# Loading a chunk's decays with it, and clearing the experts' places one expert per step

## The chip, the cores and the metric

The kernel runs on one core of one Trainium2 chip. The metric is the device time of one execution in microseconds (us). Five engines work side by side, each in its own program order: TensorE (PE in the profile, its weight loads PEld), VectorE (DVE), ScalarE (ACT), GpSimd (POOL) and SyncE (SP). Transfers are issued by SP, ACT and POOL, each into a queue of its own (the rows SPq, ACTq and POOLq show the issuing), and are carried by 16 DMA engines that all queues share.

## The reference

Three parts follow each other on 2304 tokens (4 sequences of 576) of width 512, all in float32.

```
scores = scale * q @ k^T                  # 8 heads of 64, per sequence
ret    = (scores * gamma_h ** (i - j) for j <= i, else 0) @ v
x      = ret, heads side by side                      # [2304, 512]
expert = argmax(normalise(x) @ normalise(emb).T / tau)    # one of 8
x      = gate * (relu(x @ w1[expert]) @ w2[expert])
out    = (silu(x @ w_gate) * (x @ w_val)) @ w_out
```

The factor gamma ** (i - j) is the decay. It splits into a mask inside a block of positions and powers of gamma between blocks.

## The kernel before, in words

**Attention in chunks.** Each sequence is cut into five chunks of 128, 128, 128, 128 and 64 positions, so there are 20 steps in the first stage, about the first 120 us of the span. `load_chunk(i)` brings q, k, k by rows and v of chunk i into one of six buffers `ck`: 1024 KB for a full chunk and 512 KB for the short one. `qk(i)` multiplies k and q on TensorE (line 234) and VectorE multiplies the scores by the mask `dmask_s` (line 237). `prep_chunk(i)` lets GpSimd multiply q by the decays `dq_s` (line 219, result `qd`) and k by its own powers (line 222). `pv(i)` multiplies by the state carried from earlier chunks (line 247) and by v (line 251), and ScalarE copies the result to `xT` (line 253). `state(i)` updates the carried state (line 268), which ScalarE copies to `sbd` (line 271). `rows(i)` turns the chunk back into token rows and gets the router's values (lines 280 to 287).

**Order of a step.** The order is written out by hand. In step i TensorE does `qk(i)`, `pv(i-1)`, `state(i-1)` (from the second sequence on `state(i)`) and `rows(i-2)`; step 1 also has four small transposes (line 549). The load of chunk i+5 is issued in step i, once the buffer of chunk i-1 is free. Fifteen products of ones (`warm`, line 523) stand ahead of step 0.

**The experts' places.** Tokens are sent row by row (514 floats: 512 of x, token number, gate) to a table `xs` in memory, where expert e owns a stretch of rows. Each expert later reads its first 320 rows whether they hold tokens or not, so those 8 x 320 rows are cleared first. In step 3 GpSimd fills a tile `zt` of rows with zeros and a token number behind the last token, and ScalarE issues three transfers (line 597) that write 128, 128 and 64 rows to each of the eight experts: 2056, 2056 and 1028 KB. The first tokens are sent in step 7.

**Counters of the transfers.** The transfers of SP and ACT take eight counters (DMAHW0 to DMAHW7) in turn, in the order in which the program states them, over both queues. A transfer is issued only after the previous one on its counter has landed, so it waits for the transfer eight places earlier. This wait stands on the issuing engine: on ACT it would hold the engine's arithmetic too.

**After the stage.** The eight experts (lines 681 to 712) and the gated feed-forward (lines 765 to 806) follow, both on TensorE, with weights loaded and split ahead by the same engines. The change does not touch them.

Of the kernel before, what the change touches and what calls it, by code (L numbers as in the profile page):

```python
# [4 lines left out]
F32 = mybir.dt.float32  # L5
# [4 lines left out]
ALU = mybir.AluOpType  # L10
# [20 lines left out]
# the upper word of the float64 2**-126, read as a float32  # L31
TINY = 2.0 ** -15 * 1.125
# weights come in units [128, 2, 512]: eight per expert, then three per pair of feed-forward columns
# (gate, value, output); they are kept in a ring of places
# [3 lines left out]
# products of ones that keep TensorE's clock up: before the first load is there, while the last chunk's  # L38
# experts are found, and while the tokens go through memory to the first expert
WARM = (15, 5, 42)  # L40
NTP = NT + CAP
# small constants, packed by columns
SMALL = dict(
    keep=dict(ident=P, base=E, rows=E, pos=NTI, below=E * E),
    small=dict(dk=4 * H, r8=E, tok=B * NC_ + NTI, tau=1),
# [3 lines left out]
def build(tc, main, tail, emb, wexp, dmask, dq, keep, small, lim, wffn, out):  # L49
# [24 lines left out]
    # ---------------------------------------------------------------- weights  # L74
    # Each unit is kept as hi + lo, two float32r parts that sum to it exactly. A step loads, or
    # splits, a unit of an expert or half a unit of the feed-forward's float64 weights.
# [18 lines left out]
    def split_step():  # L95
# [11 lines left out]
        else:  # L107
            # float64 bits: the float32 with their sign, exponent and leading 23 fraction bits is put
            # together from the two words, and is zero where they are below float32's least normal
# [21 lines left out]
    def feed(count=1, done=None, ahead=True):  # L131
        """Split up to `count` pieces, as far as the ring has room, with loads running ahead;
        `done`: the units that are behind us by now."""
        if done is not None:
            prog["done"] = done
        for c in range(count + 1):
            while ahead and prog["load"] < min(prog["split"] + RAW, len(steps)):
                load_step()
            if c == count or prog["split"] == len(steps) or steps[prog["split"]][0] >= prog["done"] + RING:
                return  # L140
            split_step()

    # ---------------------------------------------------------------- attention and routing
# [10 lines left out]
    dq_s = ac.tile([P, NP, S - P], F32, name="dq_s")  # L154
# [11 lines left out]
    zt = ac.tile([P, NTI, XW], F32, name="zt")  # L166
# [4 lines left out]
    sps = {}  # L171

    def load_chunk(i):
        b, c = divmod(i, NC_)
        t = cq.tile([P, 4, NP * P], F32, tag="ck", name="ck")
        if c < NC_ - 1:
            src = main[b, c].rearrange("p (a n) -> p a n", a=4)
            if i == 0:
                for h in range(2):
                    s = slice(256 * h, 256 * h + 256)  # L180
                    nc.sync.dma_start(out=t[:, 0:2, s], in_=src[:, 0:2, s])
                nc.sync.dma_start(out=dmask_s, in_=dmask)
                nc.scalar.dma_start(out=emb_s, in_=emb)
                nc.scalar.dma_start(out=small_s, in_=small)
                ck["raw0"] = t
            elif i == 1:
                nc.sync.dma_start(out=t[:, 0:2], in_=src[:, 0:2])
                nc.sync.dma_start(out=ck.pop("raw0")[:, 2:4], in_=main[0, 0].rearrange("p (a n) -> p a n", a=4)[:, 2:4])
                nc.scalar.dma_start(out=keep_s, in_=keep)
                nc.sync.dma_start(out=dq_s[:, :, 0:P], in_=dq[:, :, 0:P])  # L190
                nc.sync.dma_start(out=t[:, 2:4], in_=src[:, 2:4])
            elif i == 2:
                nc.sync.dma_start(out=t[:, 0:2], in_=src[:, 0:2])
                nc.sync.dma_start(out=t[:, 2:4], in_=src[:, 2:4])
                nc.sync.dma_start(out=dq_s[:, :, P:], in_=dq[:, :, P:])
# [3 lines left out]
        else:  # L199
            L = CH[c][1]  # L200
            nc.sync.dma_start(out=t[:, 0:2], in_=tail[b].rearrange("p (a n) -> p a n", a=2))
            ck[i] = dict(q=t[:, 0, 0:NP * L].rearrange("p (n s) -> p n s", n=NP), k=t[:, 0, NP * L:].rearrange("p (n s) -> p n s", n=NP), v=t[:, 1])

# [9 lines left out]
    def prep_chunk(i):  # L213
# [3 lines left out]
        if c:  # L217
            t["qd"] = ap.tile([P, NP, P], F32, tag="qd", name="qd", bufs=3)
            nc.gpsimd.tensor_tensor(out=t["qd"][:, :, :L], in0=t["q"], in1=dq_s[:, :, c0 - P:c0 - P + L], op=ALU.mult)
# [36 lines left out]
    def state(i):  # L256
        """The state behind chunk i, for the next one of the batch."""
# [31 lines left out]
    def last_rows():  # L289
        """The same of the last chunk, in other banks; what copies the rows is left to the caller."""  # L290
# [17 lines left out]
    class Route:  # L308
        """Expert, gate and place among the expert's rows, for chunks lo..hi-1 of a batch."""
# [5 lines left out]
        def choose(self):  # L315
# [3 lines left out]
            bc = lambda x: x.unsqueeze(2).to_broadcast([L, n, E])  # noqa: E731  # L319
# [77 lines left out]
    def turns(*chains):  # L397
        """The steps of chains, by turns."""
# [18 lines left out]
    # ---------------------------------------------------------------- tokens behind an expert's first CAP  # L417
    def count_trips(pool):
        """How many blocks of 128 tokens each expert has behind its first CAP, and their sum."""
# [6 lines left out]
    def places():  # L426
        """Where each expert's tokens begin in the order of experts, and the places of its first."""
# [12 lines left out]
    def overflow():  # L440
        total = nc.values_load(trips[0:1, E:E + 1], min_val=0, max_val=E * MAXT, skip_runtime_bounds_check_because=why)
        with tc.If(total > 0):
            with tc.tile_pool(name="op", bufs=1) as op, tc.tile_pool(name="ops", bufs=2, space=PSUM) as ops:
                padi = op.tile([P, E], I32, name="padi")
                nc.vector.tensor_scalar(out=padi, in0=base, scalar1=pos_s[:, 0:1], scalar2=None, op0=ALU.add)
                for e in range(E):
                    n = nc.values_load(trips[0:1, e:e + 1], min_val=0, max_val=MAXT, skip_runtime_bounds_check_because=why)
                    with tc.If(n > 0):
                        # rows of zeros, of no token, fill the last block
# [11 lines left out]
    def overflow_block(op, ops, e, row, cur):  # L461
        xr = op.tile([P, XW], F32, name="oxr")
        nc.sync.dma_start(out=xr, in_=xs[bass.ds(row, P), :])
        # the places of these tokens in the order of experts
# [41 lines left out]
    def place_of(pool, to, col, past):  # L506
        """Row 18 * (place % 128) + place // 128 of the table of tokens, none where `past` says so."""
# [12 lines left out]
    def warm(n, ps):  # L520
        """Products of ones, of no use but to raise TensorE's clock while it would wait."""
# [3 lines left out]
    with tc.manual_schedule():  # L525
# [5 lines left out]
        nc.vector.memset(half, 0.5)  # L531
# [368 lines left out]
```

## Time and profile before

| what | value |
|---|---|
| time, three runs | 839.88 us median (835.67, 839.88, 840.49) |
| profiled execution, span of its instructions | 837.6 us |
| TensorE busy in it | 806.3 us, 96% |
| mean granted TensorE clock | 0.983 |
| DMA engines busy, first 62 us | 0.98 |
| TensorE busy, first 62 us | 51.60 us of 62 |

The profiled execution has no time of its own in the record beside its span; the span lies 1.9 us above the fastest of the three runs and 2.3 us under their median. In the views, a row of the timeline has start, duration, engine, line, operation, tiles, count, and in brackets how long the engine stood idle before it and what released it. A row of the view by stretches has the busy time of each engine (with its count of instructions), then the granted clock as a share of full speed, the busy share of the DMA engines and GB/s.

### The profile page before, as it was taken

How to read it: one execution, taken by the hardware profiler on the slowest of the kernel's cores; microseconds unless marked ns; L12 is line 12 of the kernel's file. 1: busy time of each engine (PE TensorE's matmuls, PEld its weight loads, DVE VectorE, ACT ScalarE, POOL GpSimd, SP SyncE). 2: the span in 40 equal slices, each digit the busy share in tenths (PEclk: the TensorE clock that was granted, in tenths of full speed). 3: DMA queues.
4: the chain of work that ended last, by engine and by line, in shares of the span. 5: the costliest groups of instructions: out<-in, count | busy, mean ns of one | idle time of the engine just before them, and what ended most of it. 6: DMA issues, size and time to landing. Idle time of an engine off the chain costs nothing.

```text
span 837.6 us, 13324 instructions
## 1 busy us (share of the span) xinstructions
PE 806.3 (96%) x5337; PEld 753.1 (90%) x5337; DVE 446.2 (53%) x831; ACT 274.8 (33%) x523; POOL 163.2 (19%) x159
## 2 busy tenths in 40 slices
PE   7799887999999999999999999999999999999995
PEld 5688765999999999999999999999999999999994
DVE  2256564665565665596763753583386356323322
ACT  2234441444444445444443321331232122111110
POOL 3646551101100110122220210120021011001122
PEclk9899997999999999999999999999999999999998
DMA  9998434535645654532220210120022000000111
GB/s 325 398 359 293 126 133 143 154 133 180 194 137 164 189 158 141 158 126 98 80 76 26 76 51 1 51 76 25 1 76 76 1 26 1 0 1 29 48 76 75
DMA packets 29062, 93.83 MB, mean 112 GB/s; under 512 B 4153, under 2 KB 5818, under 8 KB 27330
## 3 DMA queue, kind: packets, MB, share of 16 engines
q1 hardware_dynamic: 22032, 77.37, 27.6%
q0 software_dynamic: 3680, 9.47, 3.0%
q10 hardware_dynamic: 3282, 6.08, 2.1%
q8 instruction: 43, 0.70, 0.3%
q14 instruction: 25, 0.20, 0.1%
HBM read 78.18 MB, written 14.73 MB: 111 GB/s over the span
## 4 chain that ended last, share of the span: by engine, by line
PE 66%; issue 14%; POOL 2%; DVE 1%; ACT 0%; POOLq 0%; DVEq 0%
PE po L798 13%; PE pg L692 9%; PE pg L693 9%; PE pg L691 9%; PE py L691 5%; PE py L692 4%; PE py L693 4%; PE ph L692 4%; PE ph L691 4%; PE ph L693 4%; POOL out L806 2%; PE ptx L681 1%; PE ph L702 0%; DVE w L117 0%; POOL w L128 0%
## 5 line engine op out<-in xcount | busy, mean ns | idle before, releaser
L692 PE MATMUL pg<-yl,w 128*128 128x384 f32 x576 | 193.0, 335 | 0.0
L693 PE MATMUL pg<-yh,w 128*128 128x384 f32 x576 | 192.7, 335 | 0.0
L691 PE MATMUL pg<-yh,w 128*128 128x384 f32 x576 | 192.7, 335 | 0.0
L798 PE MATMUL po<-w,hh 128*128 128x512 f32 x432 | 135.6, 395 | 0.0
L788 DVE TENSOR_TENSOR hf<-pg,hf 128x384 f32<-128x384 f32 x72 | 40.1, 557 | 172.5 <-PE pg L693 168.3
L128 POOL TENSOR_TENSOR w<-w,w 128x512 fp32r<-128x512 f32 x36 | 50.8, 1412 | 310.6 <-DVE hl L790 235.4
L692 PEld LDWEIGHTS pg<-yl,w 128*128 128x128 f32 x576 | 108.1, 188 | 3.0
L691 PEld LDWEIGHTS pg<-yh,w 128*128 128x128 f32 x576 | 108.1, 188 | 2.9
L693 PEld LDWEIGHTS pg<-yh,w 128*128 128x128 f32 x576 | 108.1, 188 | 0.0
L106 DVE TENSOR_TENSOR w<-raw,w 128x1024 fp32r<-128x1024 f32 x64 | 79.5, 1244 | 38.6 <-ACT w L105 37.6
L798 PEld LDWEIGHTS po<-w,hh 128*128 128x128 f32 x432 | 80.4, 188 | 13.3
L787 ACT ACTIVATE hf<-pg 128x384 f32<-128x384 f32 x72 | 35.5, 492 | 169.6 <-PE pg L693 169.6
L789 ACT ACTIVATE hh<-hf 128x384 fp32r<-128x384 f32 x72 | 37.9, 527 | 159.1 <-DVE hf L788 159.1
L798 PE MATMUL po<-w,hl 128*128 128x512 f32 x216 | 85.5, 396 | 0.0
L691 PE MATMUL py<-hh,w 128*128 128x320 f32 x256 | 81.0, 316 | 0.0
L692 PE MATMUL py<-hl,w 128*128 128x320 f32 x256 | 79.2, 309 | 0.4 <-DVE hl L709 0.4
L693 PE MATMUL py<-hh,w 128*128 128x320 f32 x256 | 79.1, 309 | 0.0
L691 PE MATMUL ph<-xh,w 128*128 128x320 f32 x252 | 78.3, 311 | 0.0
L692 PE MATMUL ph<-xl,w 128*128 128x320 f32 x252 | 78.3, 311 | 0.0
L693 PE MATMUL ph<-xh,w 128*128 128x320 f32 x252 | 78.2, 310 | 0.0
L105 ACT ACTIVATE w<-raw 128x1024 fp32r<-128x1024 f32 x64 | 66.4, 1052 | 16.8 <-PE py L693 16.7
L669 POOL DMA_INDIRECT tk<-tv,at x24 | 28.0, 1166 | 191.1 <-DVE tv L668 190.8
(127 smaller groups left out, 1166.3 us busy)
## 6 DMA issues: line engine op xcount, KB each, us to landing
raw<-wexp SPq DMA_DIRECT2D x64, 512.0 KB
raw<-wffn SPq DMA_DIRECT2D x36, 512.0 KB
ck<-main SPq DMA_DIRECT2D x13, 1024.0 KB
xs<-zt ACTq DMA_DIRECT2D x2, 2056.0 KB
xrow<-xs SPq DMA_DIRECT2D x14, 257.0 KB
ck<-main SPq DMA_DIRECT2D x5, 512.0 KB
ck<-tail SPq DMA_DIRECT2D x4, 512.0 KB
xs<-zt ACTq DMA_DIRECT2D x1, 1028.0 KB
```

The source lines that it names most:

```text
L105: nc.scalar.activation(out=w[:, 0], in_=raw, func=AF.Copy)
L106: nc.vector.tensor_tensor(out=w[:, 1], in0=raw, in1=w.bitcast(F32)[:, 0], op=ALU.subtract)
L128: nc.gpsimd.tensor_tensor(out=w[:, 1, i], in0=ff, in1=w.bitcast(F32)[:, 0, i], op=ALU.subtract)
L669: apart(tsc, nc.gpsimd.indirect_dma_start(out=tk[:, :], out_offset=bass.IndirectOffsetOnAxis(ap=at[:L, e, t:t + 1], axis=0), in_=tv[:L], i ...
L691: nc.tensor.matmul(ps, w[0], ah, start=start, stop=False)
L692: nc.tensor.matmul(ps, w[0], al, start=False, stop=False)
L693: nc.tensor.matmul(ps, w[1], ah, start=False, stop=stop)
L787: nc.scalar.activation(out=hf, in_=pss[0], func=AF.Silu)
L788: nc.vector.tensor_tensor(out=hf, in0=pss[1], in1=hf, op=ALU.mult)
L789: nc.scalar.activation(out=hh, in_=hf, func=AF.Copy)
L798: nc.tensor.matmul(po[t], h[a][:, s], w[:, c, f], start=(f == 0 and i == 0), stop=(f == 1 and i == 2))
L806: apart(osc, nc.gpsimd.indirect_dma_start(out=out[:, :], out_offset=bass.IndirectOffsetOnAxis(ap=tok[:, n:n + 1], axis=0), in_=acc[n], in_ ...
```

## The change

Four things are edited. The first chunk's q and k come in one transfer and not in two halves of columns, and its k by rows and v come right behind the mask, ahead of chunk 1. Chunks 1 and 2 come whole, where before q and k came ahead of the rest. The decays `dq` are stored chunk by chunk in memory, and each chunk's part is loaded behind the chunk (256 KB for a full one, 128 KB for the short one), where before one part of 256 KB and one of 640 KB were loaded. And the clearing is split: `zt` is 128 x 1285 zeros, made by VectorE at the start, and `clear(e)` writes the 320 rows of one expert as one contiguous block of 643 KB; `clear(0)` stands ahead of step 0 and `clear(i + 1)` at the end of step i, up to step 6. The token number behind the last token is no longer written to cleared rows.

```diff
-    dq_s = ac.tile([P, NP, S - P], F32, name="dq_s")
+    dq_s = ac.tile([P, NP * (S - P)], F32, name="dq_s")
...
-    zt = ac.tile([P, NTI, XW], F32, name="zt")
+    zt = ac.tile([P, CAP * XW // P], F32, name="zt")
...
+    def dq_of(c):
+        c0, L = CH[c]
+        return slice(NP * (c0 - P), NP * (c0 - P + L))
...
             if i == 0:
-                for h in range(2):
-                    s = slice(256 * h, 256 * h + 256)
-                    nc.sync.dma_start(out=t[:, 0:2, s], in_=src[:, 0:2, s])
+                nc.sync.dma_start(out=t[:, 0:2], in_=src[:, 0:2])
                 nc.sync.dma_start(out=dmask_s, in_=dmask)
+                nc.sync.dma_start(out=t[:, 2:4], in_=src[:, 2:4])
                 nc.scalar.dma_start(out=emb_s, in_=emb)
                 nc.scalar.dma_start(out=small_s, in_=small)
-                ck["raw0"] = t
-            elif i == 1:
-                nc.sync.dma_start(out=t[:, 0:2], in_=src[:, 0:2])
-                nc.sync.dma_start(out=ck.pop("raw0")[:, 2:4], in_=main[0, 0].rearrange("p (a n) -> p a n", a=4)[:, 2:4])
                 nc.scalar.dma_start(out=keep_s, in_=keep)
-                nc.sync.dma_start(out=dq_s[:, :, 0:P], in_=dq[:, :, 0:P])
-                nc.sync.dma_start(out=t[:, 2:4], in_=src[:, 2:4])
-            elif i == 2:
-                nc.sync.dma_start(out=t[:, 0:2], in_=src[:, 0:2])
-                nc.sync.dma_start(out=t[:, 2:4], in_=src[:, 2:4])
-                nc.sync.dma_start(out=dq_s[:, :, P:], in_=dq[:, :, P:])
             else:
                 nc.sync.dma_start(out=t, in_=src)
...
+        if 0 < i < NC_:
+            nc.sync.dma_start(out=dq_s[:, dq_of(c)], in_=dq[:, dq_of(c)])
...
         nc.vector.memset(half, 0.5)
+        nc.vector.memset(zt, 0.0)
...
+        def clear(e):
+
+            rows_e = xs[e * ER:e * ER + CAP].rearrange("r w -> (r w)")
+            nc.scalar.dma_start(out=rows_e.rearrange("(p n) -> p n", p=P), in_=zt)
+
+        clear(0)
         for i in range(N - 1):
             qk(i)
...
-            if i == 3:
-                nc.gpsimd.memset(zt, 0.0)
-                nc.gpsimd.tensor_copy(zt[:, :, D:D + 1], tok_s[:, B * NC_:].unsqueeze(2))
-                xe = xs.rearrange("(e n) w -> n e w", e=E)
-                for t, (t0, L) in enumerate(CT):
-                    nc.scalar.dma_start(out=xe[t0:t0 + L], in_=zt[:L, t].unsqueeze(1).to_broadcast([L, E, XW]))
+            if i + 1 < E:
+                clear(i + 1)
...
+    dq = np.concatenate([dq[:, :, c0 - P:c0 - P + L].reshape(P, -1) for c0, L in CH[1:]], 1)
```

The order of SP's queue at the start, before: lines 181 to 188 are q and k of chunk 0, mask, q and k of chunk 1, k by rows and v of chunk 0; lines 190 and 195 the decays; lines 191 to 194 the rest of chunks 1 and 2.

```order
L181 DMA ck<-main 128x2x256 x2
L182 DMA dmask_s<-dmask 128x1024
L187 DMA ck<-main 128x1024
L188 DMA ck<-main 128x1024 [waits DMAHW0_49]
L190 DMA dq_s<-dq 128x4x128 [waits DMAHW1_49]
L191 DMA ck<-main 128x1024 [waits DMAHW2_49]
L193 DMA ck<-main 128x1024 [waits DMAHW3_49]
L194 DMA ck<-main 128x1024 [waits DMAHW4_49]
L195 DMA dq_s<-dq 128x4x320 [waits DMAHW5_49]
L197 DMA ck<-main 128x2048 [waits DMAHW6_49]
```

The same place in the changed kernel: line 183 is q and k of chunk 0, line 185 its k by rows and v, line 190 a whole chunk, line 197 a chunk's decays.

```order
L183 DMA ck<-main 128x1024
L184 DMA dmask_s<-dmask 128x1024
L185 DMA ck<-main 128x1024
L190 DMA ck<-main 128x2048 [waits DMAHW0_49]
L197 DMA dq_s<-dq 128x512 [waits DMAHW2_49]
L190 DMA ck<-main 128x2048 [waits DMAHW3_49]
L197 DMA dq_s<-dq 128x512 [waits DMAHW4_49]
L190 DMA ck<-main 128x2048 [waits DMAHW5_49]
L197 DMA dq_s<-dq 128x512 [waits DMAHW7_49]
L194 DMA ck<-tail 128x1024 [waits DMAHW0_49]
```

What moved: q and k of chunk 1 were the third 512 KB behind the first chunk's q and k and now end with the whole of chunk 1, one transfer of 512 KB and one of 1024 KB behind the mask. The decays of chunk 3 (the third row of line 197) wait on DMAHW7, the counter of `clear(0)`.

On ACT, the place of the three clearing transfers before, in step 3 (line 597), with the arithmetic of the steps around them.

```order
L287 ACTIVATE junk,ss<-px 128x512 [waits DVE_49,PE_49,Activation_49]
L597 DMA xs<-zt 128x8x514 [waits DMAHW3_49,Pool_49]
L597 DMA xs<-zt 128x8x514 [waits DMAHW6_49]
L597 DMA xs<-zt 64x8x514 [waits DMAHW7_49]
L253 ACTIVATE xT<-po 128x512 [waits PE_49]
L271 ACTIVATE sbd_104<-st 64x4x64 [waits PE_49]
L271 ACTIVATE sbd_104<-st 64x4x64
```

On ACT in the changed kernel, from the start to step 2 (line 528 is the square of the embeddings, line 559 a clear, lines 248 and 266 are `xT` and `sbd`).

```order
L528 ACTIVATE ej,ess<-emb_s 8x512 [waits DMAHW0_49]
L559 DMA xs<-zt 128x1285 [waits DVE_49]
L559 DMA xs<-zt 128x1285 [waits DMAHW1_49]
L248 ACTIVATE xT<-po 128x512 [waits PE_49]
L266 ACTIVATE sbd_105<-st 64x4x64 [waits PE_49,Pool_49]
L266 ACTIVATE sbd_105<-st 64x4x64
L559 DMA xs<-zt 128x1285 [waits DMAHW6_49]
L248 ACTIVATE xT<-po 128x512 [waits PE_49]
L266 ACTIVATE sbd_104<-st 64x4x64 [waits PE_49]
L266 ACTIVATE sbd_104<-st 64x4x64
L282 ACTIVATE junk,ss<-px 128x512 [waits DVE_49,PE_49,Pool_49]
```

What moved: two clears now stand ahead of all of ScalarE's work on the chunks, one waiting only for `zt` and one for q and k of chunk 0 (DMAHW1), and each later clear stands alone at the end of a step.

## Rows read from the trace of the kernel before

**Rows 1.** The page: span, and TensorE's busy time and share.

```profile
span 837.6 us, 13324 instructions
PE 806.3 (96%) x5337; PEld 753.1 (90%) x5337; DVE 446.2 (53%) x831; ACT 274.8 (33%) x523; POOL 163.2 (19%) x159
```

**Rows 2.** Timeline of ScalarE in step 4: start, duration, what, idle before.

```profile
27.18 7.89 ACTq L597 DMA_DIRECT2D xs<-zt  x3
35.12 0.60 ACT L253 ACTIVATE xT<-po 128x512 f32<-128x512 f32 x1 [7.87 <-issue]
35.61 0.77 ACT L271 ACTIVATE sbd<-st 64x256 f32<-64x256 f32 x2
```

**Rows 3.** Line 597 alone: durations least, median, most in ns.

```profile
L597 ACTq DMA_DIRECT2D xs<-zt x3: 433/580/6795, 27.2 to 28.3; - x3
```

**Rows 4.** Timeline of TensorE, steps 0 to 12, merged.

```profile
7.23 1.16 PE L234 MATMUL sc<-ck 64*128 64x128 f32 x16
9.50 0.49 PE L234 MATMUL sc<-ck 64*128 64x128 f32 x2 [1.11 <-DMA ck<-main]
...
11.78 1.09 PE L251 MATMUL po<-pd,ck 128*64 128x128 f32 x16 [0.36 <-DMA ck<-main]
12.81 0.41 PE L549 MATMUL pe<-keep_s,emb_s 8*128 8x8 f32 x4
13.15 0.69 PE L268 MATMUL st<-ck 128*64 128x64 f32 x16
15.26 1.16 PE L234 MATMUL sc<-ck 64*128 64x128 f32 x16 [1.43 <-DMA ck<-main]
...
20.75 1.16 PE L234 MATMUL sc<-ck 64*128 64x128 f32 x16 [0.63 <-DMA ck<-main]
...
29.86 1.16 PE L234 MATMUL sc<-ck 64*128 64x128 f32 x16
36.48 1.94 PE L247 MATMUL po<-qd,sbd 128*128 128x64 f32 x8 [5.46 <-issue]
...
42.56 1.98 PE L234 MATMUL sc<-ck 64*128 64x128 f32 x16
...
46.88 1.16 PE L234 MATMUL sc<-ck 64*128 64x128 f32 x16
...
61.28 1.16 PE L234 MATMUL sc<-ck 64*128 64x128 f32 x16
...
65.76 1.16 PE L234 MATMUL sc<-ck 64*128 64x128 f32 x16
...
69.26 1.16 PE L234 MATMUL sc<-ck 64*128 64x128 f32 x16
```

**Rows 5.** Stretches: the five engines' busy time, granted clock, DMA share, GB/s.

```profile
33.00:34.00 1.00, 0.00 (x0) 0.00 (x0) 0.00 (x0) 0.00 (x0) 0.00 (x0) 1.00 1.04 388
34.00:35.00 1.00, 0.00 (x0) 0.00 (x0) 0.00 (x0) 0.00 (x0) 0.00 (x0) 0.53 1.05 418
...
44.00:45.00 1.00, 1.00 (x17) 0.88 (x16) 0.43 (x1) 0.26 (x2) 0.00 (x0) 0.85 1.12 308
45.00:46.00 1.00, 1.00 (x30) 1.00 (x25) 0.86 (x2) 0.40 (x1) 0.00 (x0) 1.00 0.97 312
```

**Rows 6.** Stretches of the first 50 us, for the last two columns.

```profile
2.00:10.00 8.00, 6.88 (x32) 3.03 (x30) 1.49 (x5) 2.00 (x3) 0.56 (x1) 1.00 0.96 298
10.00:20.00 10.00, 7.95 (x114) 7.07 (x114) 3.58 (x7) 2.59 (x6) 6.11 (x8) 1.00 1.04 401
...
32.00:40.00 8.00, 3.52 (x36) 3.31 (x38) 0.34 (x1) 2.31 (x6) 1.50 (x2) 0.63 1.05 387
...
44.00:50.00 6.00, 6.00 (x89) 5.45 (x88) 4.17 (x12) 2.18 (x7) 1.36 (x2) 0.98 1.01 329
```

**Rows 7.** Timeline of all engines, two rows next to each other.

```profile
8.37 0.33 SPq L194 DMA_DIRECT2D ck<-main  x1
8.38 0.43 DVE L539 COPY iec_s<-keep_s 128x512 f32<-128x512 f32 x1 [7.29 <-DMA keep_s<-keep]
```

More of the change, by code (lines that the diff above doesn't have):

```diff
@@ L44 @@
     keep=dict(ident=P, base=E, rows=E, pos=NTI, below=E * E),
-    small=dict(dk=4 * H, r8=E, tok=B * NC_ + NTI, tau=1),
+    small=dict(dk=4 * H, r8=E, tok=B * NC_, tau=1),
 )
@@ L218, in prep_chunk @@
             t["qd"] = ap.tile([P, NP, P], F32, tag="qd", name="qd", bufs=3)
-            nc.gpsimd.tensor_tensor(out=t["qd"][:, :, :L], in0=t["q"], in1=dq_s[:, :, c0 - P:c0 - P + L], op=ALU.mult)
+            nc.gpsimd.tensor_tensor(out=t["qd"][:, :, :L], in0=t["q"], in1=dq_s[:, dq_of(c)].rearrange("p (n s) -> p n s", n=NP), op=ALU.mult)
         if c < NC_ - 1:
@@ L845, in _constants @@
     ebase = np.tile(np.arange(E) * float(ER), (P, 1))
-    tok = np.zeros((P, B * NC_ + len(CT)))
+    tok = np.zeros((P, B * NC_))
     for b in range(B):
@@ L849, in _constants @@
             tok[:, b * NC_ + c] = b * S + c * P + i
-    for t in range(len(CT)):
-        tok[:, B * NC_ + t] = NT + t * P + i
     lim = ER * np.arange(E)[None, :, None] + CAP + np.arange(MAXT) * P
```

## The prediction

> **What bounds the kernel now.** I read the page first: TensorE is busy 96% of a span of 837.6 us [rows 1], so whatever the change does must show as TensorE standing still or running slowly, and only in the first stage, whose transfers alone are edited. The timelines of that stage show two places. The first is step 4. ScalarE issues the three clearing transfers from 27.18 us on, 7.89 us in all [rows 2]; two took about half a microsecond each and one 6.795 us [rows 3]. Until they are out, ScalarE's `xT` and `sbd` stand behind them: `xT` starts at 35.12 after 7.87 us idle, released by "issue", and `sbd` ends at 36.38 [rows 2]. TensorE needs that `sbd`: its next product starts at 36.48 after 5.46 us idle [rows 4]. The second place is the start. The DMA engines are full from 2 us on [rows 6], and TensorE waits for chunk loads before the products of steps 1, 2 and 3, at 9.50, 15.26 and 20.75 us [rows 4]. After that it never waits for a load in this stage.
>
> The clock belongs to the first place. The idle time began at 31.02 (29.86 + 1.16) [rows 4]; the granted clock was full until 34 us and half in the microsecond after, so it fell about 3 us into the idle time, and it was full again at about 44.3 [rows 5], 7.8 us after TensorE had resumed. In between it ran at the lower level, 1.2 of 2.4 GHz, and a group of products that takes 1.16 us took 1.98 [rows 4].
>
> **What the change takes away.** The same step in the second sequence shows step 5 without the stall: 61.28 to 65.76, 4.48 us, against 29.86 to 42.56, 12.70 us [rows 4]: 8.22 us. The step behind it: 65.76 to 69.26, 3.50, against 42.56 to 46.88, 4.32 [rows 4]: 0.82 us, the tail of the low clock. Together 9.0 us. Does the stall go? The long issue was the third of three in a row, behind 2 x 128 x 8 rows. A clear now has 128 pieces of 5140 bytes instead of 1024 of 2056, and at most two stand together, at the start, before ScalarE has work on a chunk. I take its issue at 0.43 to 0.58 us, the two short ones [rows 3]; six of them stand at ends of steps, where ScalarE waits for TensorE anyway. So I count 9.0 us gained. Were all six on the path, they would give back 6 x 0.5 = 3 us; that is an upper end. The memset of `zt` moves from GpSimd to VectorE, whose next work starts at 8.38 after 7.29 us idle [rows 7]: nothing.
>
> **What the change adds: chunk 1 arrives later.** This needs a curve of bytes. The rates were 298 GB/s from 2 to 10 us (2.38 MB) and 401 from 10 to 20 [rows 6]. Chunk 2's q and k came, with the constants of 0.16 MB, behind 3.57 MB (six times 0.524, 0.262 and the constants). The curve is there at 10 + 1.19/0.401 = 12.97, and the product started at 15.26 [rows 4], 2.3 us later. Chunk 3, behind 5.80 MB, gives 18.5 and 20.75 [rows 4], again 2.3. So a load is usable 2.3 us after the curve passes its last byte.
>
> In the changed queue chunk 1 ends with 0.16 + 3 x 0.524 + 1.05 = 2.78 MB of loads. Of the clears (0.658 MB each) two are issued at about 5 us, once the embeddings' square is done and q and k of chunk 0 are there; they share the engines with the loads. How many bytes of them pass ahead of chunk 1 no row shows, so I bound it. With none, and 401 GB/s from 2 us on because the pieces are larger: 2 + 6.9 + 2.3 = 11.2 us. With both, at the rates of before: 10 + (4.09 - 2.38)/0.401 + 2.3 = 16.6. I take one clear ahead, at the rates of before: 10 + (3.44 - 2.38)/0.401 + 2.3 = 14.9, between the ends because the two queues each have work waiting. The nearest row is that of the small constants in ACT's queue: 105 KB issued by 2 us landed only when VectorE's copy and SP's next load went on, at 8.37 [rows 7], so that queue is not served first. The Trainium skill says in "DMA: Bandwidth & Descriptors", section "Queues, rings and completion order", that each DMA engine goes round between the queues that have work, a packet at a time. By that rule the clears take turns with the loads from the moment they are issued; equal in bytes, this puts both ahead of chunk 1, and the sum would be -1.2 us instead of my -3.0 (the second rival). The late constants agree with it so far that ACT's queue is not served ahead.
>
> TensorE then idles from 8.39 (7.23 + 1.16) [rows 4] to 14.9, 6.5 us, longer than the 5.46 after which the clock fell. So I expect the low clock from about 11.4 until 14.9 + 7.8 = 22.7. From `qk(1)` to `qk(2)` the work is 1.16 + 1.09 + 0.41 + 0.69 = 3.3 us (less a little overlap), from `qk(2)` to `qk(3)` 20.75 - 15.26 - 0.63 = 4.9 [rows 4], together 8.0 at full clock. In 7.8 us at half rate 3.9 are done, the other 4.1 follow: `qk(3)` at 26.8 instead of 20.75, **6.0 us lost**. Loads are not later than that: chunk 3 is behind 3.44 + 0.66 + 2 x 0.262 + 2 x 1.05 = 6.7 MB, curve 20.8, usable at 23.1 (24.8 with a third clear).
>
> What is queued behind the late chunk on TensorE is the first chunk's `pv` and the transposes; behind those ScalarE's `xT` and `sbd` and the third clear. All have slack until the next `qk`.
>
> Then loads and clears together: by step 7 chunks 0 to 7 (7.86 MB), constants, mask and decays (1.6) and seven clears (4.6), 14.1 MB. After 20 us (6.4 MB) at 387 GB/s they take 19.8 us, at the 329 of the mixed stretch 23.4 [rows 6]; usable at 42.1 or 45.7. TensorE reaches step 7 at 26.8 + 9.11 (20.75 to 29.86) + 4.48 + 3.50 = 43.9, against 46.88 before [rows 4]. So the loads could cost up to 1.8 us more; I take 0.
>
> **The sum.** -9.0 + 6.0 = -3.0 us. The profiled execution goes from 837.6 to 834.6; the median of the runs, 2.3 us above that span, from 839.88 to **836.9**.
>
> **Rivals.** *The loads lose nothing* (chance 0.20). If the larger pieces run at 401 GB/s at once and the clears take the gaps, chunk 1 is usable at 11.2, the idle time is 2.8 us and the clock stays: `qk(3)` at 19.2 by work, about 21 by its load. Then only the 9.0 us count, less some tenths: 831 to 832. For it: the first rate, 298, goes with 1 KB and smaller pieces that are gone. Against it: the engines were already busy 0.96 then [rows 6].
>
> *Both clears first* (0.15). Chunk 1 at 16.6, low clock to 24.4, `qk(3)` at 28.5: 7.8 us lost, and the 1.8 us of late loads on top in part: 838.7 to 840.5, no change. The Trainium skill's rule of turns (the section named above) leads here; no row yet shows how the turns share out the bytes.
>
> *Every step waits for its transfers* (0.07, the slower side). A clear at the end of step i waits on ScalarE for the transfer eight places earlier, among them the loads of chunks 2, 4 and 7. If reads and writes together run at the 298 GB/s of the worst row [rows 6] up to step 7 (14.1 MB: 2.38 by 10 us, 39.3 us for the rest, 51.6 with the lag), ScalarE is held by loads as it now is by the issue, step 7 comes 4.7 us later than its 46.88 [rows 4], and the low clock, which lasts 7.8 us beyond the last long wait, costs 3.9 more: 848.5. It begins where the rate from 20 us on falls under 356 GB/s (7.7 MB in the 21.6 us until step 7 at 43.9, less the lag), and turns the sign at 312, where step 7 is back at 46.9. For it: 329 stands in one row. Against it: 387 stands in the row where the clears ran almost alone [rows 6].
>
> *The stall stays* (0.08). If a single clear still held ScalarE for microseconds in step 3 or 4, the gain falls away and the loss stays: 839.9 + 6.0 = 846. Against it: the short issues of 0.43 and 0.58 us were the larger transfers [rows 3].
>
> **The numbers.** My forecast has 0.50, with its own range of 833.5 to 840. The range of eight in ten, 831 to 844, takes in the first rival and both clears first, and leaves out most of the last two and the far ends. About 1%, 8.4 us, is what a measurement of this kernel can tell from no change, its three runs lying 4.8 us apart. Faster by over 1% means under 831.5: half of the first rival and a little of the forecast's low end, 0.12. Slower by over 1% means above 848.3: the third rival's upper half and a share for the fourth, 0.06. Within 1%: 0.82.
>
> **What would show it.** The `sbd` copies of step 4 follow `xT` with no "issue" wait of microseconds, and the granted clock is full between 32 and 44 us: that is the 9.0. `qk(1)` starts near 14.9 instead of 9.50, waiting for `ck<-main`, and the clock reads half behind it: that is the 6.0. If `qk(1)` starts before 12 us with a full clock the first rival holds; if TensorE waits for `ck<-main` or for ScalarE in steps 4 to 8, the third. I am wrong altogether if the time changes behind the first stage, which I cost at nothing because no instruction there is edited.

## The result and the profile after

| | median | lowest to highest | ratio to before, 95% interval |
|---|---|---|---|
| before, five runs | 838.29 us | 835.67 to 840.49 | |
| changed, five runs | 830.94 us | 829.77 to 833.24 | 0.9912 [0.9892, 0.9933] |

That is 7.35 us less, where 3.0 less was forecast, and just under the range's lower end of 831. Three later comparisons of the same two kernels gave 0.9918 [0.9897, 0.9938], 0.9939 [0.992, 0.9958] and 0.9926 [0.9902, 0.995], the last two against the same runs of the kernel before: 5 to 7 us. The forecast's own ratio, 836.9 to 839.88 or 0.9964, lies outside all four intervals.

The page of the changed kernel, to [rows 1]: 9.2 us less span in this execution, TensorE with 5.3 us less work (less of it at the low clock) and 3.9 us less idle time. Steps 5 to 7 give 9.0 of the 9.2 us, the start costs 2.1, and 2.3 come behind step 7, where this execution had 6.8 us of low clock and the one of before 13.6 (the table under E12 to E16); the medians differ by less.

```profile
span 828.4 us, 13328 instructions
PE 801.0 (97%) x5337; PEld 748.7 (90%) x5337; DVE 449.6 (54%) x832; ACT 274.8 (33%) x523; POOL 162.3 (20%) x157
```

The timeline of ScalarE in steps 3 and 4 (start, duration, what, idle before and its releaser), to [rows 2]:

```profile
28.63 0.60 ACT L282 ACTIVATE junk<-px 128x512 f32<-128x512 f32 x1 [1.16 <-DVE xr L279]
28.68 0.34 ACTq L559 DMA_DIRECT2D xs<-zt  x1
...
30.46 0.60 ACT L248 ACTIVATE xT<-po 128x512 f32<-128x512 f32 x1 [1.14 <-PE po L246]
30.95 0.77 ACT L266 ACTIVATE sbd<-st 64x256 f32<-64x256 f32 x2
```

The clear is issued in 0.34 us beside the square of `junk`, and `xT` waits for TensorE and no longer for "issue". All eight clears are like that (least, median, most in ns), to [rows 3]:

```profile
L559 ACTq DMA_DIRECT2D xs<-zt x8: 338/338/380, 2.8 to 41.0; - x8
```

The timeline of TensorE, to [rows 4]:

```profile
7.17 1.16 PE L229 MATMUL sc<-ck 64*128 64x128 f32 x16
13.36 2.03 PE L229 MATMUL sc<-ck 64*128 64x128 f32 x16 [5.03 <-DMA ck<-main]
15.32 1.83 PE L246 MATMUL po<-pd,ck 128*64 128x128 f32 x16
...
18.04 1.16 PE L229 MATMUL sc<-ck 64*128 64x128 f32 x16
...
22.83 1.16 PE L229 MATMUL sc<-ck 64*128 64x128 f32 x16
```

Chunk 1 comes 3.86 us later than before (9.50 to 13.36), step 3 only 2.08 us later (20.75 to 22.83). Steps 5, 6, 7 and 8 start at 31.93, 36.41, 39.91 and 45.67: steps 5 and 6 take 7.98 us together, where they took 17.02 [rows 4], 9.04 less. The stretches, to [rows 6] and [rows 5] (five engines' busy time, granted clock, DMA share, GB/s):

```profile
2.00:10.00 8.00, 6.34 (x30) 2.69 (x28) 0.63 (x2) 2.00 (x3) 1.52 (x2) 1.00 0.92 324
10.00:20.00 10.00, 6.64 (x75) 6.02 (x76) 5.42 (x11) 1.35 (x3) 5.16 (x8) 0.83 1.02 418
...
44.00:50.00 6.00, 6.00 (x79) 5.49 (x80) 4.27 (x19) 2.38 (x8) 1.07 (x2) 1.00 1.02 418
13.00:13.50 0.50, 0.14 (x2) 0.14 (x4) 0.30 (x1) 0.00 (x0) 0.00 (x0) 0.95 1.10 448
13.50:14.00 0.50, 0.50 (x6) 0.50 (x8) 0.00 (x0) 0.00 (x0) 0.00 (x0) 0.50 1.03 421
16.50:17.00 0.50, 0.50 (x8) 0.39 (x4) 0.20 (x1) 0.00 (x0) 0.50 (x1) 0.64 0.92 361
17.00:17.50 0.50, 0.50 (x10) 0.40 (x8) 0.00 (x0) 0.30 (x1) 0.50 (x2) 1.00 1.15 463
33.00:34.00 1.00, 1.00 (x10) 0.97 (x8) 0.88 (x2) 0.63 (x2) 1.00 (x2) 1.00 1.03 429
```

The clock fell at about 13.5 and was back at 16.9, 3.5 us after TensorE had resumed, where 7.8 were taken. With clears of 5140-byte pieces beside the loads the engines moved 418 GB/s from 44 to 50 us, where 329 stood before [rows 6].

### The profile page after: what moved, and what is told of

It is laid out like the page before. It is cut to its first block, busy times and chain, and to the rows that moved or that the text cites. A ratio compares the mean times of both kernels' runs of the same rounds, so it can differ in the third digit from the quotient of the medians.

```text
span 828.4 us, 13328 instructions
## 1 busy us (share of the span) xinstructions
PE 801.0 (97%) x5337; PEld 748.7 (90%) x5337; DVE 449.6 (54%) x832; ACT 274.8 (33%) x523; POOL 162.3 (20%) x157
## 4 chain that ended last, share of the span: by engine, by line
PE 67%; issue 14%; POOL 2%; DVE 1%; ACT 0%; POOLq 0%; DVEq 0%; ACTq 0%
PE po L796 13%; PE pg L690 9%; PE pg L691 9%; PE pg L689 9%; PE py L689 5%; PE py L690 4%; PE py L691 4%; PE ph L689 4%; PE ph L690 4%; PE ph L691 4%; POOL out L804 2%; PE ptx L679 1%; PE ph L700 0%; DVE w L117 0%; POOL w L128 0%
```

## The experiments

Ratios are to the kernel before on the same chip. The first four ran on one chip, E5 to E8 on a second, E9 to E12 on a third, E13 to E16 on a fourth; the kernel before had medians of 838.05, 835.72, 838.54 and 834.82 us on them. Steps are told by the start of their `sc` products.

**E1, the split clearing alone**, with the loads of before.

```diff
-    zt = ac.tile([P, NTI, XW], F32, name="zt")
+    zt = ac.tile([P, CAP * XW // P], F32, name="zt")
...
+        nc.vector.memset(zt, 0.0)
...
+        clear(0)
...
-            if i == 3:
-                ...
-                    nc.scalar.dma_start(out=xe[t0:t0 + L], in_=zt[:L, t].unsqueeze(1).to_broadcast([L, E, XW]))
+            if i + 1 < E:
+                clear(i + 1)
```

> The kernel before with the clearing of the change alone (one contiguous 643 KB block per expert, one per step, the first two ahead of the work on the chunks); its order of loads is kept. Theory (the whole gain is ScalarE no longer held in step 4, 9.0 us at step 7; the change's load order costs 2.1 us of it): 829 to 831 us against 838.3, ratio about 0.990, no issue on ScalarE over 0.6 us, and qk(1) later than 9.50 only by what the two early clears take, under 2 us. Rival (the gain needs the larger loads, whose higher rate of 420 GB/s lets the clears pass): 834 us or more, with TensorE waiting for chunk loads in steps 4 to 8.

833.98 us, 0.9957 [0.9939, 0.9976], neither range. The stall is gone and TensorE waits for nothing from 20 to 60 us, but the two early clears delay chunk 1 by 3.5 us against before (TensorE's timeline):

```profile
12.98 2.08 PE L234 MATMUL sc<-ck 64*128 64x128 f32 x16 [5.07 <-DMA ck<-main]
```

At the 405 GB/s of 8 to 13 us in this run that is about 1.4 MB, both clears (1.32 MB). The view of transfers for these 5 us (pieces, MB, share; q1 is SP's queue with the loads, q10 ScalarE's with the clears):

```profile
q10 hardware_dynamic: 274, 1.18, 57.5%
q1 hardware_dynamic: 471, 0.84, 44.2%
```

The Trainium skill ("DMA: Bandwidth & Descriptors", section "Queues, rings and completion order") has each engine go round its queues a packet at a time; this run agrees so far that the two queues moved side by side, though not in equal bytes. Here the clock was low for 10.2 us, and step 5 came at 34.64.

**E2, the changed loads alone**, with the three clears of before.

```diff
...
-        clear(0)
...
-            if i + 1 < E:
-                clear(i + 1)
+            if i == 3:
+                nc.gpsimd.memset(zt, 0.0)
+                ...
+                    nc.scalar.dma_start(out=xe[t0:t0 + L], in_=zt[:L, t].unsqueeze(1).to_broadcast([L, E, XW]))
```

> The changed kernel with the clearing of before (three transfers in step 3, rows of 2056 bytes). Theory: the stall stays, xT of step 4 stands about 7.9 us behind the issue, and the load order costs 2 us: 838 to 842 us, ratio 1.000 to 1.005. Rival (the larger loads free the DMA engines, so the third issue is held for less): the issue under 4 us and a time under 836.

839.36 us, 1.0014 [0.9997, 1.0031], as the theory said: the stall stays (6.8 us, where 7.9 was expected). Chunk 1 was there at 11.31, 2 us earlier than in the changed kernel. On ScalarE's timeline:

```profile
28.89 0.43 ACTq L592 DMA_DIRECT2D xs<-zt  x1
29.27 0.19 ACT L282 ACTIVATION_READ_ACCUMULATOR junk<-px 128x1 f32 x1
29.36 6.88 ACTq L592 DMA_DIRECT2D xs<-zt  x2
36.29 0.60 ACT L248 ACTIVATE xT<-po 128x512 f32<-128x512 f32 x1 [6.82 <-issue]
```

**E3, three long clears**: the kernel before, with its three clears at the same place writing the same places, in pieces of 5140 bytes (384, 384 and 256 of them, where there were 1024, 1024 and 512). The bytes are the same; the copy of the token number into `zt` is left out, as in the changed kernel.

```diff
-    zt = ac.tile([P, NTI, XW], F32, name="zt")
+    zt = ac.tile([P, CAP * XW // P], F32, name="zt")
...
-                nc.gpsimd.tensor_copy(zt[:, :, D:D + 1], tok_s[:, B * NC_:].unsqueeze(2))
-                xe = xs.rearrange("(e n) w -> n e w", e=E)
-                for t, (t0, L) in enumerate(CT):
-                    nc.scalar.dma_start(out=xe[t0:t0 + L], in_=zt[:L, t].unsqueeze(1).to_broadcast([L, E, XW]))
+                xe = xs.rearrange("(e r) w -> e (r w)", e=E)[:, 0:CAP * XW].rearrange("e (p n) -> p e n", p=P)
+                for e0, n in ((0, 3), (3, 3), (6, 2)):
+                    nc.scalar.dma_start(out=xe[:, e0:e0 + n], in_=zt.unsqueeze(1).to_broadcast([P, n, CAP * XW // P]))
```

> The kernel before, in its own order, with the same three transfers of the clearing in step 3 and the same 5.26 MB, but in pieces of 5140 bytes instead of 2056: 384, 384 and 256 pieces instead of 1024, 1024 and 512. If the number of pieces waiting in ACT's queue holds the third issue, it takes under 1 us now, TensorE doesn't stall in step 4 and the time falls by about 9 us, to 829 to 831 (ratio 0.990). Rival: the bytes waiting in the queue hold it; then it still takes 4 to 7 us and the time is 836 or more.

838.76 us, 1.0003 [0.9985, 1.0022]. The theory held for the hold and missed the time. On ScalarE's timeline the hold of 6.8 us is gone, with fewer and longer pieces of the same bytes; the second and third issue still took 2.0 us together, where under 1 us was expected of the third:

```profile
26.03 0.43 ACTq L596 DMA_DIRECT2D xs<-zt  x1
26.41 0.19 ACT L287 ACTIVATION_READ_ACCUMULATOR junk<-px 128x1 f32 x1
26.50 2.00 ACTq L596 DMA_DIRECT2D xs<-zt  x2
28.54 0.60 ACT L253 ACTIVATE xT<-po 128x512 f32<-128x512 f32 x1 [1.93 <-PE st L268]
```

Step 7 started at 37.20 instead of 46.88, 9.68 us earlier; the whole gain was given back behind it. On GpSimd's timeline the first sending of tokens waits for the clears:

```profile
56.73 1.21 POOL L393 DMA_INDIRECT xs<-xr,slot  x1 [15.83 <-DMA xs<-zt]
```

GpSimd stands 15.83 us with the chunks' preparation behind it, TensorE waits 4.67 us for it (`st`, line 268, at 59.08), and the clock is low for 6.8 us from 57 and for 3.4 from 74. In the changed kernel, whose clears are issued from 2.8 to 41 us, the first sending starts at 51.66, 5 us earlier, and TensorE waits for nothing there. Clears that start late save the start and hold the first sending.

**E4, chunk 1's q and k first**: the changed kernel with these two ahead of chunk 0's k by rows and v.

```diff
-                nc.sync.dma_start(out=t[:, 2:4], in_=src[:, 2:4])
+                ck["raw0"] = t
...
+            elif i == 1:
+                nc.sync.dma_start(out=t[:, 0:2], in_=src[:, 0:2])
+                nc.sync.dma_start(out=ck.pop("raw0")[:, 2:4], in_=main[0, 0].rearrange("p (a n) -> p a n", a=4)[:, 2:4])
+                nc.sync.dma_start(out=t[:, 2:4], in_=src[:, 2:4])
```

> The changed kernel with q and k of chunk 1 loaded right behind the mask, ahead of k by rows and v of chunk 0, as before; the rest of chunk 1 comes last. Theory (the start loses 2.1 us to step 3 because TensorE idles 5 us for the whole of chunk 1 and then runs 3.3 us at the lower clock): qk(1) at 9.5 to 11.5 us, the clock stays full, step 3 at 20.8 to 21.3 instead of 22.83 and the time 1.5 to 2 us under the changed kernel, 829 us. Rival (chunk 2's load, behind the same bytes, sets step 2 at about 18 us whatever comes first): step 3 at 22.5 or later and no gain, 831.

833.43 us, 0.9934 [0.991, 0.9958]. The rival held: step 1 starts at 8.61, but TensorE then waits 2.17 us for VectorE's `pd` within the step and 3.44 us for chunk 2, at 17.84, with 6.8 us of low clock, and step 5 is at 34.34. The order of the loads moves the wait, since the bytes are the same.

**E5, the changed kernel again.** Nothing edited.

> The changed kernel once more, nothing edited. Theory: the start's loss is 2.1 us because the low clock lasted only from 13.5 to 16.7 us, and how long it lasts after TensorE resumes follows from the program, so a second profile has chunk 1's products near 13.4 us, step 3's near 22.8 and the clock full again before 18 us; time 830 to 832. Rival: the length of the low stretch is a matter of the single execution (the traces so far show 2.9 to 9.2 us from resuming to full clock); then this profile may show it full only at 20 to 23 us and step 3's products at 24.5 to 26, and the runs' times scatter by some 3 us for that reason.

828.31 us, 0.9918 [0.9897, 0.9938]. The rival held for the clock: the same program was at the low level from 12.3 to 22.5 us (stretches, columns as above):

```profile
12.00:12.50 0.50, 0.00 (x0) 0.00 (x0) 0.50 (x2) 0.00 (x0) 0.00 (x0) 0.77 1.07 431
12.50:13.00 0.50, 0.00 (x0) 0.00 (x0) 0.50 (x2) 0.00 (x0) 0.00 (x0) 0.50 1.03 417
...
21.00:22.00 1.00, 1.00 (x7) 1.00 (x7) 0.94 (x2) 0.00 (x0) 0.16 (x1) 0.50 1.08 420
22.00:23.00 1.00, 1.00 (x11) 0.78 (x12) 0.00 (x0) 0.00 (x0) 0.95 (x1) 0.75 1.09 437
```

and its timeline of TensorE has step 3 at 25.17 and not at 22.83, though chunk 1 came no later:

```profile
13.06 2.08 PE L229 MATMUL sc<-ck 64*128 64x128 f32 x16 [5.31 <-DMA ck<-main]
...
18.55 2.08 PE L229 MATMUL sc<-ck 64*128 64x128 f32 x16
...
25.17 1.16 PE L229 MATMUL sc<-ck 64*128 64x128 f32 x16
```

**E6, the gap filled**: the changed kernel with 22 products of ones behind step 0's products.

```diff
             qk(i)
+            if i == 0:
+                warm(22, ps_1.tile([P, 512], F32, tag="px", name="warm"))
```

> The changed kernel with 22 more products of ones behind step 0's products, so that TensorE has no idle time from 8.3 to 13.4 us. Theory: the clock no longer falls, the work of step 1 and 2 takes 3.3 us where it took 4.7, and step 2's products come at 16.7 instead of 18.0 unless chunk 2's load is later; 1.4 us less, 829 to 830. Rival: chunk 2's load is the bound of step 2 (usable at 16 to 18 us by the curve of bytes), the clock stays full and TensorE waits for the load, gain under 0.5 us: 830.5 to 831.5.

831.25 us, 0.994 [0.9917, 0.9963], not faster than E5 beside it. The clock stayed full until 81 us, and now the loads set steps 2 and 3, as the rival said (timeline of TensorE):

```profile
17.69 1.16 PE L229 MATMUL sc<-ck 64*128 64x128 f32 x16 [1.71 <-DMA ck<-main]
...
23.19 1.16 PE L229 MATMUL sc<-ck 64*128 64x128 f32 x16 [0.63 <-DMA ck<-main]
```

Chunk 3 is usable at 23.2, where 23.1 was forecast: with a full clock the loads alone put step 3 2.4 us later than in the first profile of before (20.75). The 0.97 us that TensorE then waits for ScalarE's `junk` in step 3 lets step 5 start at 33.33. In the profiled execution the clock was low for 10.2 us from 81, behind an idle time of 2.11 us.

**E7, pairs**: the changed kernel with the clears two by two, from step 1 on.

```diff
-        clear(0)
...
-            if i + 1 < E:
-                clear(i + 1)
+            if 1 <= i <= E // 2:
+                clear(2 * i - 2)
+                clear(2 * i - 1)
```

> The changed kernel with no clear ahead of the loop and the eight clears in pairs at the ends of steps 1 to 4. Theory: the clears that are issued before 5 us delay chunk 1, so its products come at 11.3 us instead of 13.4 (as with the loads alone), step 3's at 22 to 23, and no pair holds ScalarE (each issue 0.3 to 0.4 us): 829 to 831. Rival: the clears only move, the pairs beside the loads of chunks 2 to 6 make steps 2 to 5 wait for transfers by 2 to 4 us or the first sending of tokens waits for the clears as with the three long ones: 832 to 835.

827.65 us, 0.9915 [0.9896, 0.9933], no different from E5; at the 838.29 us from which the theory's 829 to 831 were reckoned the ratio makes 831.2. Without early clears chunk 1 is there at 10.83, but step 3 starts at 23.75, not at 22 to 23, behind 10.2 us of low clock; step 5 starts at 32.86 and the first sending at 51.65. One of the eight issues took 1.14 us, where 0.3 to 0.4 were expected; ScalarE's next `xT` waited for TensorE, not for it.

**E8, three long clears, sending later**: E3 with the first sequence's tokens sent four steps later. **E9, E10 and E11** are the same edit on the kernel before, on the changed kernel and on E7.

```diff
-                    at_step(i + 1 + (n if b < B - 2 else n // 2), lambda r=r, n=n: r.scatter(n))
+                    at_step(i + 1 + (n if b < B - 2 else n // 2) + (4 if b == 0 else 0), lambda r=r, n=n: r.scatter(n))
```

> The kernel before with the three clears in pieces of 5140 bytes, and the first sequence's tokens sent four steps later. Theory: in the run with the three long clears the 9.7 us gained at step 7 were given back because GpSimd stood 15.8 us (40.9 to 56.7) on the first sending of tokens, which waited for the clears, with the chunks' preparation behind it; with the sending later, no low clock between 57 and 77 us, and most of the gain stays: 828.5 to 831. Rival: the gain is given back by something else (loads behind the clears, the sendings that now come together): 835 to 839, with TensorE waiting in steps 8 to 14 all the same.

827.95 us, 0.9916 [0.9892, 0.9939]. GpSimd's hold is gone and the gain of E3 stays: step 7 starts at 34.58, and there is no low clock between 18 and 119 us. So the gain can be had with the loads of before and without early clears.

> The kernel before with one edit: the first sequence's tokens are sent four steps later. The control for the run with three long clears and the later sending. Theory: the stall of step 4 stays (its 9.0 us were taken away by the longer pieces, not by the later sending), TensorE's idle time of 2.1 us at step 16 shrinks to about 1 us with the sendings out of its way and the low clock that follows it in some executions goes; 0.5 to 2 us faster than before, 0.3% at most. Rival: the later sending alone is what made that run 7 us faster; then this one is 6 to 8 us faster too, 0.991 to 0.993.

844.36 us, 1.0055 [1.0029, 1.008]: slower, so both were wrong. The stall stays (5.86 us of "issue"), and the other idle time, which the expectations call step 16, is longer, not shorter. Counted by the starts of the `sc` products it lies in step 14, as the 2.12 us in the first profile of before did (TensorE's timeline, before and E9):

```profile
85.43 2.18 PE L280 MATMUL px<-iec_s,xT 128*128 128x136 f32 x8 [2.12 <-ACT junk L287]
...
87.45 2.18 PE L280 MATMUL px<-iec_s,xT 128*128 128x136 f32 x8 [3.28 <-ACT junk L287]
```

ScalarE's `junk` waits there for VectorE, whose split of an expert's weights took 3.63 us (VectorE's timeline):

```profile
82.27 3.63 DVE L106 TENSOR_TENSOR w<-raw,w 128x1024 fp32r<-128x1024 f32 x1 [2.59 <-ACT w L105]
```

In it fall two multiplications of GpSimd (timeline of GpSimd):

```profile
82.51 1.30 POOL L219 TENSOR_TENSOR qd<-ck,dq_s 128x512 f32<-128x512 f32 x1
83.75 1.06 POOL L222 TENSOR_TENSOR ck<-ck,small_s 128x512 f32<-128x512 f32 x1
```

In E8 the same split falls beside a sending and takes 1.25 us:

```profile
73.60 1.25 DVE L106 TENSOR_TENSOR w<-raw,w 128x1024 fp32r<-128x1024 f32 x1 [1.86 <-ACT w L105]
```

> The changed kernel with the first sequence's tokens sent four steps later. Theory: the changed kernel still has GpSimd wait 6.6 to 7.5 us at the first sending and TensorE wait 2.1 us at step 16, behind which the clock falls in some executions; without both, 1 to 3 us less than the changed kernel: ratio to before 0.988 to 0.990. Rival: nothing on TensorE's path hangs on the sending, the time is that of the changed kernel, 0.991 to 0.993.

> The changed kernel with the clears in pairs at steps 1 to 4, and the first sequence's tokens sent four steps later. Theory: both gains stand beside each other, the start as in the run with the pairs (step 5's products at 32.9 us, 1 to 1.4 us earlier than in the changed kernel run beside it) and no idle time over 1.2 us at step 16; ratio to before 0.986 to 0.989. Rival: the pairs gain nothing measurable over the changed kernel and the sending neither: 0.990 to 0.993.

837.18 us, 0.9975 [0.9959, 0.9991], and 836.35 us, 0.9978 [0.9961, 0.9995], outside what theory and rival said in both expectations: most of the gain is lost, with 3.28 and 3.27 us of idle time in step 14 and the split at 3.6 us in both. Idle time in step 16 grew too, from 1.0 us in the changed kernel to 2.3. Together that is 2.5 us; what else was lost was not traced. Later sending is no gain by itself; in E8 it freed GpSimd and happened to shift the split away from GpSimd's arithmetic.

**E12 to E16, both kernels again.** Nothing edited: E12, E14 and E16 are the kernel before, E13 and E15 the changed one.

> The kernel before once more, nothing edited, beside the other three on one chip. Ratio to before 1.000 within its interval. Theory: the long issue and the low clock behind it, 10.2 us long, stand in every execution (step 4 takes 12.7 us here too), while the short low stretch at step 16 (3.4 us in the first profile) and the one at the first expert (10.2 us) differ by steps of 3.4 us from execution to execution. Rival: the low stretches of the kernel before are always the same, 10.2, 3.4 and 10.2 us.

> The changed kernel, nothing edited, another profile. Theory: three low stretches (start, first expert, the end), the one at the start 3.4 or 10.2 us long, the one at the first expert 6.8, none at step 16; the step from 5 to 7 takes 8.0 us. Rival: step 16's 2.1 us idle time is followed by a low clock here as often as in the kernel before.

> The kernel before, nothing edited, another profile. Theory: 10.2 us of low clock behind step 4, and behind step 6 some 3 us more of it than in the changed kernel (at step 16 in some executions, 6.8 to 10.2 us at the first expert), which is 1.5 us of the difference of the medians. Rival: behind step 6 both kernels have the same low clock, and the rest of the difference is idle time.

> The changed kernel, nothing edited, a further profile. Expected as of the other one of this kernel: 3.4 or 10.2 us of low clock at the start, 6.8 at the first expert, none at step 16.

> The kernel before, nothing edited, a further profile. Expected as of the other one of this kernel: 10.2 us of low clock behind step 4, behind step 6 on average 3 us more of it than in the changed kernel.

E12 1.0002 [0.9986, 1.0019], E14 0.9988 [0.9968, 1.0008], E16 0.9998 [0.9965, 1.0031], E13 0.9939 [0.992, 0.9958], E15 0.9926 [0.9902, 0.995]. With the two first profiles there are four executions of each kernel (us; the low clock is summed over 1-us stretches, without the end behind 810):

| kernel | step 5 starts | steps 5 to 7 take | rest of the span | low clock before step 8 | low clock behind it |
|---|---|---|---|---|---|
| before | 29.86 | 22.78 | 785.0 | 10.2 | 13.6 |
| before, E12 | 28.98 | 22.60 | 782.8 | 10.2 | 6.8 |
| before, E14 | 29.25 | 21.97 | 778.2 | 6.8 | 6.8 |
| before, E16 | 29.82 | 22.84 | 781.2 | 10.2 | 13.6 |
| changed | 31.93 | 13.74 | 782.7 | 3.4 | 6.8 |
| changed, E5 | 34.27 | 13.75 | 779.0 | 10.2 | 6.8 |
| changed, E13 | 34.22 | 13.75 | 781.4 | 10.2 | 13.6 |
| changed, E15 | 31.49 | 13.74 | 781.3 | 3.4 | 10.2 |
| mean, before | 29.48 | 22.55 | 781.8 | 9.4 | 10.2 |
| mean, changed | 32.98 | 13.75 | 781.1 | 6.8 | 9.4 |

The means give +3.5 at the start, -8.8 in steps 5 to 7 and -0.7 behind them: -6.0 us. My theory that the kernel before has some 3 us more of low clock behind step 6 fell (10.2 against 9.4); the rival held in that. The lengths named for single stretches missed as well: the one behind step 4 was 6.8 us in E14, and the one at the first expert 10.2 us in E13 and E15. Step 14's idle time of 2.1 us (the expectations' step 16) was followed by a low clock in two of the four executions of before and in one of the changed kernel.

## Why the prediction was wrong

**What bounds the kernel, and the 9.0 us.** Right, in place and in size. The two steps gave back 9.04 us in the first profile and 8.8 in the means; `xT` has no "issue" wait and the clock is full from 32 to 44 us. The bytes that stand in the queue do not hold the issue: E3 left them as they were, cut 2560 pieces to 1024, and the hold of 6.8 us went. That leaves the pieces; whether their number in the queue or the short length of each counts was not separated, nor the shape of the third transfer (64 partitions before, 128 in E3). The six later clears cost nothing; each is issued beside ScalarE's arithmetic.

**The 6.0 us at the start.** This is the step that failed: a mis-sized term, with the mechanism right. Chunk 1 is late, TensorE idles for 5 us, the clock falls; but step 3 lost 2.08 us in the first profile, and the start 3.5 in the mean of four. Two numbers under it were off.

The first is the landing of chunk 1: 12.85 to 13.36 us in four profiles, not 14.9. The bytes ahead of it were right. In the view of transfers for 2 to 12 us of the changed kernel (columns as in E1) SP's queue has moved 2.63 MB, and chunk 0, mask and chunk 1 are 2.62; ScalarE's has moved 0.79, which is 0.14 of constants and 0.65 of clears, one clear as chosen:

```profile
q1 hardware_dynamic: 586, 2.63, 72.4%
q10 hardware_dynamic: 423, 0.79, 21.0%
```

The rates were 324 and 418 GB/s, not the 298 and 401 of before that were carried over; by them the forecast's 3.44 MB are there at 10 + (3.44 - 2.59)/0.418 = 12.0 us, not at 12.6. And the chunk was used 1.3 us behind that, not 2.3. Against E2 and E7, which have no early clears, it is 1.5 to 2.5 us late, 0.6 to 1.1 MB at 418 GB/s.

Turns of equal bytes, as in the second rival, would have put both clears ahead. From 8 to 12 us the two queues moved about as many pieces, not as many bytes; a row of a whole chunk is a piece of 8192 bytes, one of a clear 5140:

```profile
q1 hardware_dynamic: 146, 0.94, 58.9%
q10 hardware_dynamic: 155, 0.66, 39.8%
```

In E4, whose early loads have rows of 4096 bytes, 244 and 242 pieces from 8 to 13 us were 0.90 MB of loads and 1.08 of clears. So the longer pieces of the loads may be what let chunk 1 pass the second clear; no run edits them alone.

The second is the length of the low clock, 3.5 us after resuming in the first profile. It was taken as 7.8 us after resuming, from the one stretch of step 4 [rows 5], as if it were the same each time. In the first profile the landing makes 1.5 us of the 3.9 that the term was too large, the clock the other 2.4. The same unedited program had it 3.4 us long in two executions and 10.2 in two, and step 5 starts at 31.71 in the mean of the former and 34.25 of the latter. Two more stretches of low clock stood in the trace of before, 3.4 us at 85 us and 10.2 us at 133, and were not read; they would have given the range. A term of 2 to 5 us in place of 6.0 makes -7 to -4.

**Later loads at 0, and the stage behind.** Right: no wait for a transfer in steps 4 to 8 of the changed kernel, 418 to 422 GB/s where 329 was feared, and -0.7 us in the rest of the span, less than its scatter of 7 us between executions.

**The rivals.** "The loads lose nothing" had the right size of time for the first comparison (831 to 832) and the wrong reason: chunk 1 was late and the clock did fall. "Both clears first" is near to what E1 shows with the loads of before, but its landing of 16.6 us did not come in any run, and its loss was forecast from the same 7.8 us. The other two did not come.

**What stays open**: what decides between 3.4, 6.8 and 10.2 us of low clock. In E5 as in the first profile TensorE resumed at 13.1 to 13.4 us and had no idle time until step 3, so its work behind the fall does not tell them apart. Where the clock was low for 3.4 us (first profile, E15) it fell within 0.3 us of TensorE's resuming, where it was low for 10.2 (E5, E13) 0.8 and 1.0 us ahead of it; but in E6 it fell 1.4 us behind the resuming, at 81.0 us, and was low for 10.2 all the same. The -7.35 of the first comparison against -6.0 in the means lies within the intervals.

## What to carry to other kernels

Count the pieces of a transfer, and what is queued ahead of it, before you put its issue on an engine that has arithmetic to do: here the third of three issues took 6.8 us behind 2048 pieces of 2056 bytes, the second and third together 2.0 us with pieces of 5140, and a single block of 128 such pieces mostly 0.3 us. Where a clear is started early to be out of the way it takes its bytes from the loads that run then, where it is started late the first user waits: price both ends (E1 and E3). Read every low stretch of the clock in the trace before using one of them as a length; with the scatter seen here, give such a term as a range.

## What was not expected of the hardware

The low stretches before the last 20 us had lengths of 3.4, 6.8, 10.2 and once (E9) 13.7 us by the granted clock, and differed between executions of one program; an idle time of 2.1 us was followed by one or by none. A VectorE operation of 1.25 us took 2.46 us in the kernel before and 3.63 in E9, when one (with the end of another) and two GpSimd multiplications of 1.1 to 1.3 us fell into it: it seems to stand still while they run (E8, beside a sending: 1.25). The Trainium skill ("SBUF — State Buffer", section "SBUF: two separate sides") says that a GpSimd operation that reads SBUF and a VectorE operation with two inputs there can't hold their shared ports together, and that the one that starts first keeps them; the rows agree on the waiting, but by the recorded starts of E9 VectorE was first (82.27 against 82.51) and was lengthened all the same; recorded spans on GpSimd are rough, so the order is not sure. A transfer's issue on ScalarE's queue runs beside its arithmetic where it is short: in the changed kernel a clear is issued at 28.68 us during `junk`, from 28.63.
